# One pair of half parts moved from the expert loop into the tail's branch

## The chip, the cores and the metric

The kernel runs on one core of a Trainium2 chip. A core has five engines with queues of their own: TensorE (PE in the profile; PEld is its weight load), VectorE (DVE), ScalarE (ACT), GpSimd (POOL) and SyncE (SP), which here issues nearly all of the loads. [...] The metric is the device time of one execution in microseconds (us); for the kernel before it is the median of three runs, 2620.4 us (2619.55 to 2623.47).

## The reference

Two stages follow each other. The first is a gated attention unit on 8 sequences of 2496 tokens with width 256: scores from `z` (64 wide), a squared relu in place of a softmax, and a gate `u`. The second sends each of the 19968 tokens to one of 8 experts, by a hash of its id, and applies that expert's two layers:

```python
scores = scale * np.matmul(z, z.transpose(0, 2, 1))
attn = np.maximum(scores, 0.0) ** 2
x = (u * np.matmul(attn, v)).reshape(N, D)            # N = 19968, D = 256
expert_idx = token_ids * np.int64(2654435761) % np.int64(E)   # E = 8
for e in range(E):
    mask = expert_idx == e
    h = np.maximum(x[mask] @ w1[e], 0.0)              # w1[e]: 256 x 1024
    out[mask] = h @ w2[e]                             # w2[e]: 1024 x 256
```

The multiplier is 1 modulo 8, so the expert is the id modulo 8. Inputs come from a fixed seed, all in float32.

## The kernel before

Attention fills the first 1510 us or so and isn't touched. While it runs, the token ids are sorted into slots: `places()` counts the tokens of each expert and gives each token a row in `x_rows`, in DRAM. `idx` holds, for each slot, the token that sits in it, or N (19968) for an empty slot; a store with N as its row is dropped.

The slots are divided into units of work of three kinds:

- 32 whole blocks (`NW`) of 512 tokens of one expert (work numbers 0 to 31),
- 27 parts (`NP`) of 128 tokens of one expert (32 to 58),
- pairs of half parts of 64 tokens, where each half has an expert of its own (59 and on). With `NH` = 8 halves there are four pairs in the loop, 59 to 62. `MH` = 9 halves can be needed at most, so one more pair, 63, is in the branch.

Which expert a unit has is read on the device (`eb_i`). A number that the device also computes, `extra`, says how far the units are used: twice the number of parts (27 at least) plus the number of half parts, and N more if tokens of the first block came too late and it has to be redone. Units are thus counted in halves: the 27 parts are the first 54, and a part beyond the 27th takes both halves of a pair.

For a unit the steps are:

1. `load_x` (L699): four loads of its rows on SP. There are three buffers (`LOADS`), used in turn.
2. `load_w` (L717, L718): per expert, one read of `eb_i`, four loads for `w1` (256 KB each) and one for `w2` (1024 KB), all on SP. There are four sets of weight buffers (`w_buf`); `w_free` is a list from which a unit takes one set per expert, and into which it puts them back when its down products are written. A pair takes two sets.
3. `turn_x` (L730): VectorE transposes x.
4. The up product: `ups` for a whole block (L834) or `ups_of_part` (L855). ScalarE and VectorE take turns with the relu (L840, L842). For a part or a pair the result lies the wrong way round, and sixteen transposes on VectorE (L861) follow.
5. `down` (L869): the down product, a copy on ScalarE (L877) and a store by GpSimd (L882) with the token numbers as rows.

`run()` works through a list of units. In step i it issues the x load of unit i+2, the up product of unit i with the turn of unit i+1's x after its second bank, the down product of unit i-1, and the weight load of unit i+2. If unit i-1 is a part, its down product comes after all of unit i's up product; if it is a whole block and unit i a part, the up product of the part comes first. The first step of a call of `run` has no down product of an earlier unit. The order of instructions on each engine is the order in which this code issues them (`tc.manual_schedule()`).

The list alternates whole blocks with parts and pairs: 31 couples and then whole block 31. The first call of `run` does all but the last three units, with the loads of the next two. Then the number is read into registers of four engines, and a branch (L938) does, only when more than 62 halves are used, a second run of block 0 and the pair 63; their outputs go to `o_all`, which is cleared beforehand (L811) and stored after the branch in any case (POOL isn't in the branch). Last, the three remaining units are run.

Of the kernel before, what the change touches and what calls it, by code (L numbers as in the profile page):

```python
# [24 lines left out]
def kernel(  # L25
# [10 lines left out]
    nc = tc.nc  # L36
# [8 lines left out]
    P = 128  # L45
# [16 lines left out]
    BLK = 512  # L62
    HALF = P // 2
    NW = -(-(N - E * (BLK - 1)) // BLK)
    NP = (N - NW * BLK) // P - 1
    NH = E

    MH = max(NH, (N - NW * BLK + E * (HALF - 1)) // HALF - 2 * NP)
    NT = NP + -(-MH // 2)
# [615 lines left out]
    AHEAD = 1  # L685
    LOADS = 3
# [3 lines left out]
    def slots(j):  # L690

        return (j * BLK // P, BLK // P) if j < NW else (NW * BLK // P + j - NW, 1)

    def load_x(j, k):

        c, n = slots(j)
        xg[j] = xg_buf[k][:, 0:n * P // Q, :]
        for r in range(NQ):
            nc.sync.dma_start(  # L699
                xg[j][ts(r, Q)],  # L700
                x_dram[ds(c * P, n * P), ts(r, D // NQ)].rearrange("(k i) d -> i k d", i=Q))

    def experts(j):

        k = j - NW - NP
        return [j] if k < 0 else [*range(j + k, min(j + k + 2, NB))]

    def load_w(j):
        sets[j] = [w_free.pop(0) for _ in experts(j)]
        w1[j], w2[j] = [], []  # L710
        for k, x in zip(sets[j], experts(j)):
            w1[j].append(w_buf[k][0].rearrange("p (h f) -> p h f", h=DP))
            w2[j].append(w_buf[k][1].rearrange("p (c d) -> p c d", c=FP))
            e = nc.sync.value_load(eb_i[0:1, x:x + 1], min_val=0, max_val=E - 1)
            for r in range(NQ):
                rows = moe_w1[ds(e, 1), ts(r, D // NQ)].rearrange("one d f -> (one d) f")
                nc.sync.dma_start(w1[j][-1][ts(r, Q), :, :], rows.rearrange("(h i) f -> i h f", i=Q))  # L717
            nc.sync.dma_start(  # L718
                w2[j][-1], moe_w2[ds(e, 1)].rearrange("one f d -> (one f) d").rearrange("(c p) d -> p c d", p=P))

    def turned_x(tile, k):
        return tile[:, ts(k, XW), :].rearrange("p c d -> p (c d)").rearrange("p (k h i) -> p k h i", h=DP, i=Q)

    def turn_x(j, k):
        n = slots(j)[1] * P // Q
        xT[j] = xT_buf[k][:, 0:n]
        if slots(j)[1] == 1:

            xT[j] = xT[j].rearrange("p k h i -> p (k h i)").rearrange("p (h k i) -> p k h i", h=DP, i=Q)
        nc.vector.transpose(xT[j], xg[j].rearrange("p k (h i) -> p k h i", i=Q))  # L730
# [77 lines left out]

    opool = pool("opool", 4)
    o_all = vpool.tile([P, T, D], F32, name="v_sb")  # L810
    nc.gpsimd.memset(o_all[:, 0:BLK // P * AHEAD + (MH - NH + 1) // 2, :], 0.0)  # L811
    xT_buf.append(turned_x(o_all, T // XW - 1))

    w_free.append(len(w_buf))
# [48 lines left out]
    def down(j, t, later):  # L863
        ps = acc_ps.tile([P, D], F32, name="o_ps", tag="acc")
        for f in range(FP):
            for h, w in enumerate(w2[j]):

                cols = halves(j, h)
                nc.tensor.matmul(ps[cols, :], hT[j][f][:, ts(t, P)][:, cols], w[:, f, :],  # L869
                                 start=(f == 0), stop=(f == FP - 1), skip_group_check=True)  # L870
        k = slots(j)[0] + t
        if later is not None:
            o = o_all[:, len(later), :]
            later.append((o, again[:, k:k + 1] if j < AHEAD else idx[:, k:k + 1]))
        else:
            o = opool.tile([P, D], F32, name="o_sb")[:]
        nc.scalar.copy(o, ps[:])  # L877
        if later is None:
            store(o, once[:, k:k + 1] if j < AHEAD else idx[:, k:k + 1])
# [8 lines left out]
    def run(work, first, last, loads, later=None):  # L888

        for i in range(first, last + 1):  # L890
            if i < last and i + 2 < loads:
                load_x(work[i + 2], (i + 2) % LOADS)
            do = [lambda t=t: down(work[i - 1], t, later) for t in range(slots(work[i - 1])[1])] if i > first else []
            banks = [*range(BLK // P * 2 if work[i] < NW else 2)] if i < last else []
            if first < i == AHEAD:

                while do:
                    do.pop(0)()
            up = (ups_of_part if work[i] >= NW else ups)(work[i]) if i < last else None

            late = i > first and work[i - 1] >= NW
            for k in banks:
                next(up)
                if k == (banks[-1] if i < AHEAD else 0 if i == AHEAD else 1) and AHEAD <= i + 1 < max(last, loads):
                    turn_x(work[i + 1], (i + 1) % LOADS)
                if k % 2 == 1 and not late:
                    for _ in range(-(-len(do) * 2 // (len(banks) - k + 1))):
                        do.pop(0)()
            if i < last:
                next(up, None)  # L910
            for f in do:
                f()
            if i > first:
                w_free.extend(sets.pop(work[i - 1]))
            if i < last and i + 2 < loads:
                load_w(work[i + 2])
# [3 lines left out]

    NU = NP + NH // 2
    assert NU == NW - 1 and NH % 2 == 0 and MH <= NH + 1
    small = [*range(NW, NW + NP)]
    for k in range(NH // 2):
        small.insert((k + 1) * NU // (NH // 2 + 1), NW + NP + k)
    work = [j for pair in zip(range(NW - 1), small) for j in pair] + [NW - 1]
    NM = len(work) - 3
    load_w(work[1])  # L930
    load_x(work[1], 1)
# [1 line left out]
    n_used = nc.values_load(extra[0:1, 0:1], min_val=1, max_val=NB + N, engines=[  # L933
        mybir.EngineType.PE, mybir.EngineType.Activation, mybir.EngineType.DVE, mybir.EngineType.SP])

    nc.gpsimd.drain()  # L936
    later = []
    with tc.If(n_used > 2 * NP + NH):  # L938
        for j in [*range(AHEAD), *range(NW + NU, NW + NT)]:
            load_x(j, (NM + 2) % LOADS)  # L940
            load_w(j)
            turn_x(j, (NM + 2) % LOADS)
            run([j], 0, 1, 0, later)
    for o, rows in later:
        store(o, rows)
    run(work, NM, len(work), len(work))
# [30 lines left out]
```

## Time and profile before

| what | value |
|---|---|
| median of three runs | 2620.4 us |
| the profiled execution, its own time | 2619.45 us |
| its span, first to last instruction | 2617.4 us |
| TensorE busy | 2610.0 us, 8105 matmul records |
| VectorE, ScalarE, GpSimd busy | 1453.5, 584.2, 607.4 us |
| granted TensorE clock, whole span | 1.000 |
| DMA, mean over the span | 124 GB/s |
| one whole block and one part, per round of the loop | 34.43 us |

A float32 matmul leaves two records in the trace, so a whole block's down product of 32 matmuls is shown with x64. Matmuls are pipelined and the ends of their records are modelled, so a record reaches past the start of the next; distances between starts are the better measure. In a row of the timeline the bracket tells how long the engine had been idle before and what ended that. Queues of a transfer are named by the engine that issues it (SPq). A transfer's landing time is counted from its issue.

In the text below, a gap is time in which TensorE could have gone on but waits.

### The profile page before, as it was taken

The numbers are of one execution on the slowest core, as the hardware profiler recorded it, in microseconds if no ns is written. First come the engines' busy times: TensorE is split into PE (matmuls) and PEld (weight loads), VectorE is DVE, ScalarE is ACT, GpSimd is POOL, SyncE is SP. The second block draws the span as 40 slices with busy tenths as digits, with TensorE's granted clock in tenths as the row PEclk, the third lists the DMA queues.
The fourth block names the chain that finished last, engine by engine and source line by source line (L and its number), as shares of the span: only waits on it lengthen the run. The fifth ranks groups of instructions, "written<-read, shape, count | busy, mean of one in ns | idle before, by whom it ended". The sixth has DMA issues, their size and how long they took to land.

```text
span 2617.4 us, 26062 instructions
## 1 busy us (share of the span) xinstructions
PE 2610.0 (100%) x8105; PEld 1441.9 (55%) x8105; DVE 1453.5 (56%) x3285; ACT 584.2 (22%) x1268; POOL 607.4 (23%) x668
## 2 busy tenths in 40 slices
PE   9999999999999999999999999999999999999999
PEld 4444444444454444444444456666666666666666
DVE  7977768767766866767758633333333333333332
ACT  5214213232233123133142111111111111111111
POOL 1342233133242331333222211111111111111112
PEclk9999999999999999999999999999999999999999
DMA  4443333333422423323423387667657667667641
GB/s 121 121 120 83 84 98 93 89 95 88 117 71 77 124 71 98 102 75 95 118 55 87 104 208 182 153 165 203 162 144 196 166 159 187 152 161 198 171 126 48
DMA packets 446556, 324.91 MB, mean 124 GB/s; under 512 B 267308, under 2 KB 408765, under 8 KB 446416
## 3 DMA queue, kind: packets, MB, share of 16 engines
q1 hardware_dynamic: 424672, 281.48, 42.2%
q0 software_dynamic: 20592, 41.09, 4.9%
q8 instruction: 65, 1.06, 0.2%
q10 hardware_dynamic: 1152, 0.66, 0.1%
q14 instruction: 75, 0.61, 0.1%
HBM read 233.29 MB, written 66.75 MB: 115 GB/s over the span
## 4 chain that ended last, share of the span: by engine, by line
PE 58%; issue 35%; POOL 6%; DMA 0%; POOLq 0%; DVE 0%; ACTq 0%; DVEq 0%
PE acc L359 49%; PE s_ps L232 7%; POOL out_dram L882 6%; PE acc L367 2%; POOLq L882 0%; PE z_ps L176 0%; DMA zn<-in_z_dram 0%; DMA x_way<-x_q 0%; DMA x_sb<-x_way 0%; POOL x_rows L637 0%; DVE hT L842 0%; DVE x_sb L395 0%; POOLq L972 0%; POOLq L936 0%; POOL v_sb L811 0%
## 5 line engine op out<-in xcount | busy, mean ns | idle before, releaser
L359 PE MATMUL acc<-a,v_sb 128*128 128x512 f32 (+1 forms) x1760 | 765.9, 592 | 0.0
L270 DVE STREAM_TRANSPOSE m<-a 32x512 f32<-32x512 f32 (+1 forms) x896 | 603.8, 674 | 18.8 <-ACT a L248 3.4
L359 PEld LDWEIGHTS acc<-a,v_sb 128*128 128x128 f32 x1760 | 342.2, 196 | 390.5 <-issue 375.2
L359 PE MATMUL acc<-m,v_sb 128*128 128x512 f32 (+1 forms) x1280 | 527.2, 571 | 0.0
L842 DVE TENSOR_SCALAR hT<-h_ps 128x512 f32<-128x512 f32 x159 | 109.8, 691 | 684.5 <-PE h_ps L834 494.4
L869 PE MATMUL o_ps<-m,hT 128*128 128x256 f32 (+1 forms) x2064 | 446.9, 379 | 0.0
L240 ACT ACTIVATE a<-s_ps 128x512 f32<-128x512 f32 (+3 forms) x456 | 202.1, 585 | 1034.3 <-PE s_ps L232 1034.3
L869 PEld LDWEIGHTS o_ps<-m,hT 128*128 128x128 f32 (+1 forms) x2064 | 382.3, 188 | 75.9 <-issue 24.3
L359 PEld LDWEIGHTS acc<-m,v_sb 128*128 128x128 f32 x1280 | 251.2, 196 | 271.7 <-issue 268.2
L834 PE MATMUL h_ps<-v_sb,m 128*128 128x512 f32 x832 | 361.4, 592 | 0.7 <-PEq L938 0.7
L882 POOL DMA_INDIRECT out_dram<-o_sb,idx x155 | 151.5, 977 | 905.2 <-ACT o_sb L877 897.3
L395 POOL TENSOR_TENSOR x_sb<-x_sb,u_sb 128x256 f32<-128x256 f32 (+1 forms) x156 | 108.0, 720 | 909.3 <-DMA x_sb<-x_way 909.3
L296 DVE STREAM_TRANSPOSE a<-a 32x128 f32<-32x128 f32 (+2 forms) x1360 | 282.2, 239 | 9.9
L834 PEld LDWEIGHTS h_ps<-v_sb,m 128*128 128x128 f32 x832 | 158.0, 190 | 189.7 <-issue 188.5
L248 ACT ACTIVATE a<-a 128x512 f32<-128x512 f32 (+1 forms) x480 | 229.5, 640 | 0.0
L861 DVE STREAM_TRANSPOSE hT<-hT 32x256 f32<-32x256 f32 x496 | 214.9, 433 | 6.5
L375 DVE STREAM_TRANSPOSE x_q<-acc 128x512 f32<-128x512 f32 (+1 forms) x80 | 56.6, 708 | 281.3 <-PE acc L359 281.2
L877 ACT COPY o_sb<-o_ps 128x256 f32<-128x256 f32 x159 | 59.2, 372 | 585.6 <-PE o_ps L869 585.6
L232 PE MATMUL s_ps<-zT 64*128 64x512 f32 (+1 forms) x960 | 188.4, 536 | 0.0
L840 ACT ACTIVATE hT<-h_ps 128x512 f32<-128x512 f32 x159 | 94.8, 597 | 392.6 <-PE h_ps L834 349.7
L637 POOL DMA_INDIRECT x_rows<-x_sb,slot_i x160 | 157.8, 986 | 69.4 <-issue 35.8
L625 POOL DMA_INDIRECT slot_tokens<-token,addr x160 | 155.9, 974 | 50.9 <-issue 48.2
(121 smaller groups left out, 926.4 us busy)
## 6 DMA issues: line engine op xcount, KB each, us to landing
m<-in_moe_w_dram SPq DMA_DIRECT2D x204, 256.0 KB, 6.0
m<-in_moe_w_dram SPq DMA_DIRECT2D x51, 1024.0 KB, 6.0
m<-stage SPq DMA_DIRECT2D x320, 64.0 KB, 2.0
v_sb<-in_v_dram SPq DMA_DIRECT2D x32, 512.0 KB, 4.8
u_sb<-in_u_dram SPq DMA_DIRECT2D x32, 512.0 KB, 4.9
x_way<-x_q SPq DMA_DIRECT2D x128, 128.0 KB, 2.5
x_sb<-x_way SPq DMA_DIRECT2D x32, 512.0 KB, 4.0
v_sb<-x_rows SPq DMA_DIRECT2D x128, 128.0 KB, 6.6
```

The source lines that it names most:

```text
L232: nc.tensor.matmul(ps[:, lo:n], zT[b][h, ts(t, P)], zT[b][h, ds(g * G * P + lo, n - lo)], start=True, stop=True)
L240: nc.scalar.activation(a, ps[:, lo:n], AF.Relu)
L248: nc.scalar.activation(a, a, AF.Square, scale=1.0 / S)
L270: nc.vector.transpose(o, x[ts(r, Q), 0:m * G, ts(c, Q)].rearrange("p (i s) q -> p i s q", s=G))
L296: return n * Q, lambda: nc.vector.transpose(out, in_)
L359: nc.tensor.matmul(acc[h][:, 0:queries(g)], v_sb[b][:, t, h::2], squares(b, g, t), start=(k == 0), stop=(k == TM - 1), skip_group_check=True)
L625: st = nc.gpsimd.indirect_dma_start(out=slot_dram[:, None], out_offset=bass.IndirectOffsetOnAxis(ap=addr[0:n, c:c + 1], axis=0), in_=token ...
L637: st = nc.gpsimd.indirect_dma_start(out=x_dram[:, :], out_offset=bass.IndirectOffsetOnAxis(ap=slot_i[0:width(c % T), c:c + 1], axis=0), in ...
L834: nc.tensor.matmul(ps[:], w1[j][0][:, c, ts(f, P)], xT[j][:, :, c, :], start=(c == 0), stop=(c == DP - 1))
L861: nc.vector.transpose(turned[ts(c, Q), :, ts(r, Q)], rows[ts(r, Q), :, ts(c, Q)])
L869: nc.tensor.matmul(ps[cols, :], hT[j][f][:, ts(t, P)][:, cols], w[:, f, :], start=(f == 0), stop=(f == FP - 1), skip_group_check=True)
L882: st = nc.gpsimd.indirect_dma_start(out=out[:], out_offset=bass.IndirectOffsetOnAxis(ap=rows, axis=0), in_=o, in_offset=None, bounds_check ...
```

## The change

Pair 62, the last of the four pairs of the loop, is taken out of it. It gets an outer branch of its own in the tail, entered when more than 60 halves are used; the branch over 62 halves, with block 0 and pair 63, is put inside of it. The pair's x and weights are loaded and its x is turned ahead of the branch, whether it is entered or not. Its output goes to `o_all`, which gets one more row, and is stored with the others after the branch.

The loop's list becomes 30 couples and then whole blocks 30 and 31. The three remaining pairs are spread anew over it. The last three units, which run after the branch, were whole block 30, a part and whole block 31; now they are a part, whole block 30 and whole block 31.

```diff
-    nc.gpsimd.memset(o_all[:, 0:BLK // P * AHEAD + (MH - NH + 1) // 2, :], 0.0)
+    nc.gpsimd.memset(o_all[:, 0:BLK // P * AHEAD + (MH - NH + 1) // 2 + 1, :], 0.0)
...
-    NU = NP + NH // 2
-    assert NU == NW - 1 and NH % 2 == 0 and MH <= NH + 1
+    last_pair = NW + NP + NH // 2 - 1
+    NU = last_pair - NW
+    assert NU < NW and NH % 2 == 0 and MH <= NH + 1
     small = [*range(NW, NW + NP)]
-    for k in range(NH // 2):
-        small.insert((k + 1) * NU // (NH // 2 + 1), NW + NP + k)
-    work = [j for pair in zip(range(NW - 1), small) for j in pair] + [NW - 1]
+    for k in range(NH // 2 - 1):
+        small.insert((k + 1) * NU // (NH // 2), NW + NP + k)
+    work = [j for pair in zip(range(NU), small) for j in pair] + [*range(NU, NW)]
     NM = len(work) - 3
...
     later = []
-    with tc.If(n_used > 2 * NP + NH):
-        for j in [*range(AHEAD), *range(NW + NU, NW + NT)]:
-            load_x(j, (NM + 2) % LOADS)
-            load_w(j)
-            turn_x(j, (NM + 2) % LOADS)
-            run([j], 0, 1, 0, later)
+    load_x(last_pair, (NM + 2) % LOADS)
+    load_w(last_pair)
+    turn_x(last_pair, (NM + 2) % LOADS)
+    with tc.If(n_used > 2 * NP + NH - 2):
+        run([last_pair], 0, 1, 0, later)
+        with tc.If(n_used > 2 * NP + NH):
+            for j in [*range(AHEAD), *range(last_pair + 1, NW + NT)]:
+                load_x(j, (NM + 2) % LOADS)
+                load_w(j)
+                turn_x(j, (NM + 2) % LOADS)
+                run([j], 0, 1, 0, later)
     for o, rows in later:
         store(o, rows)
     run(work, NM, len(work), len(work))
```

## Prediction

> **What bounds the kernel now.** I read the page's busy times first, then TensorE's waits, then the timeline in order of time: a usual stretch, the tail, and what the stores of the pairs moved. Busy time:
>
> ```profile
> PE 2610.0 (100%) x8105; PEld 1441.9 (55%) x8105; DVE 1453.5 (56%) x3285; ACT 584.2 (22%) x1268; POOL 607.4 (23%) x668
> ```
>
> TensorE (PE) is busy for all but 7.4 of 2617.4 us. Its waits (engine and line, for whom, us in total, times, longest):
>
> ```profile
> PE warm L652 <- POOL zero L102: 1.2, 1, 1.2
> PE h_ps L834 <- PEq L938: 0.7, 1, 0.7
> PE z_ps L176 <- DMA zn<-in_z_dram: 0.5, 1, 0.5
> ```
>
> Two are at the kernel's start. In 1,100 us of expert work there is one, 0.7 us at the branch of L938, so TensorE's own stream sets the end: an edit gains by taking matmuls out of it and costs by opening a gap in it. Now a pair of half parts among its neighbours (start us, us, engine, line, what):
>
> ```profile
> 1716.66 13.90 PE L834 MATMUL h_ps<-v_sb,m 128*128 128x512 f32 x32
> 1730.40 3.62 PE L869 MATMUL o_ps<-zT,hT 128*128 128x256 f32 x16
> 1733.94 3.65 PE L855 MATMUL h_ps<-m,v_sb 128*64 128x512 f32 x16
> 1737.53 14.08 PE L869 MATMUL o_ps<-m,hT 128*128 128x256 f32 x64
> 1751.44 13.90 PE L834 MATMUL h_ps<-v_sb,zn 128*128 128x512 f32 x32
> 1765.27 3.67 PE L869 MATMUL o_ps<-m,hT 128*64 128x256 f32 x32
> ```
>
> A pair's up product (1733.94) and its down product (1765.27) lie 31 us apart, with 28 us of a whole block's matmuls between. What that cover hides is in the tail, where a part goes the same way:
>
> ```profile
> 2532.03 13.98 PE L869 MATMUL o_ps<-m,hT 128*128 128x256 f32 x64
> 2532.24 0.69 DVE L842 TENSOR_SCALAR hT<-h_ps 128x512 f32<-128x512 f32 x1 [6.19 <-PE h_ps L855]
> 2532.84 1.24 DVE L730 STREAM_TRANSPOSE v_sb<-v_sb 128x1024 f32<-128x1024 f32 x1
> 2534.00 7.13 DVE L861 STREAM_TRANSPOSE hT<-hT 32x256 f32<-32x256 f32 x16
> ...
> 2545.85 3.62 PE L869 MATMUL o_ps<-zT,hT 128*128 128x256 f32 x16
> 2550.17 13.97 PE L834 MATMUL h_ps<-v_sb,m 128*128 128x512 f32 x32 [0.70 <-PEq L938]
> ```
>
> After the up product VectorE needs a relu, the turn of the next block's x, and sixteen transposes until 2541.13; only then may the down product start. TensorE does a whole block's down product meanwhile.
>
> **Is the pair needed with this data?** I counted by the kernel's rules from the reference's fixed inputs. Tokens per expert: 2506, 2446, 2582, 2478, 2498, 2473, 2434, 2551. The 32 whole blocks fall 4, 4, 5, 4, 4, 4, 4, 3, leaving 458, 398, 22, 430, 450, 425, 386, 1015. Parts, (rest+63)>>7: 4, 3, 0, 3, 4, 3, 3, 8, so 28; half parts (the next lower bit): 0, 1, 1, 1, 0, 1, 1, 0, so 5. The number that the branch tests is 2x28+5 = 61. The old test, over 62, fails (as the trace shows), so no block is redone. The new outer test, over 60, holds; the inner, over 62, fails. The pair's body runs. The trace backs the counts: the pairs should hold 119, 14+22, 46+41 and 2 tokens, at 1 KB a row 0.12, 0.04, 0.09 and 0.00 MB. The software queue in the 11 us or so after each pair's down product (packets, MB, share):
>
> ```profile
> q0 software_dynamic: 48, 0.12, 2.6%
> ...
> q0 software_dynamic: 48, 0.04, 1.0%
> ...
> q0 software_dynamic: 48, 0.09, 2.0%
> ...
> q0 software_dynamic: 48, 0.00, 0.3%
> ```
>
> So the change removes no matmul. It moves a pair out of a covered place.
>
> [...] the same 128x256 shape that takes 379 ns later takes
>
> ```profile
> L652 PE MATMUL warm<-zero x6: 634/634/796, 1.2 to 3.5; 128*128 128x256 f32 x6
> ```
>
> [...] TensorE's took 236 ns here, 3.4 us ahead of the matmuls that it follows, hidden.
>
> **The change, part by part.**
>
> *Removed from the loop.* The pair with its slots: two rounds took 34.78 (1716.66 to 1751.44) and 34.79 us against 34.43 with full parts, so a pair costs 34.78+34.79-2x34.43 = 0.71 more than a part, whose two products are 3.43+3.45: 7.6 us. All of it comes back in the tail: net 0. The three other pairs move to other rounds, with the same cover: 0.
>
> *Loads moved ahead of the branch.* SP issues the pair's four x loads and twice four w1 loads and one w2, after all loads of the loop. The first expert takes the weight buffers of the block before the last one run, so only its w2 waits, for that part's down product (my t=0, 2528.4 in the old trace). Behind it on SP stand the second expert's w1 loads: issued from about t=1.7 to 4.9 (gap 0.96 from x loads to w1, and 3.17 for four, at 2515.01). 2 MB at the 220 GB/s seen in these stretches land by about t=11; TensorE comes for them at t=13.9, when the last block's down product ends. Cover 3 us; if it fails, each us late costs one. The second w2 waits for that down product, is issued at about 14.3 and, with 6.0 us to land, is there at 20.5; needed at 26. The pair's x is turned before that on an idle VectorE (0.45 us). 0 in all.
>
> *The exposed body.* Between up and down product now stands nothing. From the old tail: the relu starts at 2532.24, the transposes can follow 0.60 later (no turn of x between) and take 7.13, to 2539.97; I add 0.3 for signal and first weight load (two weight loads took 0.41 here). TensorE could have gone on at 2532.03: 8.24 us of gap. Nothing else on VectorE or ScalarE stands in it.
>
> *The clock.* [...] and 0 if the clock doesn't drop. I take 2.0.
>
> *Tail's order.* One pair fewer makes the rest after the branch part, whole, whole instead of whole, part, whole. The part has no down product to overlap: the next whole block's up product needs its x turned, which VectorE does after the part's relu: 2532.84+1.24+0.3 = 2534.38 against 2532.03, 2.35 us of gap. It was under a 14 us down product before. The part's own transposes (7.13) now hide under that up product (13.9): 0. The last block's x (after VectorE's pass through the branches, t=26) and weights (after TensorE's, t=32) land by about 47, needed after 55: 0. The rest has the old matmuls and the old end.
>
> *Branches.* The skipped inner branch takes over the old 0.70. The entered outer one runs ahead under matmuls; its exit jump I put at 0.2 (0 to 1.5).
>
> *One store more and a memset of 1536 instead of 1280 elements* on POOL (0.98; 1.2 x 1536/1280 = 1.44): POOL was idle 3.27 us after the memset, and stores are no one's wait. 0.
>
> Sum: 8.24+2.35+2.0+0.2 = +12.8. Profiled span 2617.4+12.8 = 2630.2, the profiled time 2619.45+12.8 = 2632.2. The shown median, 2620.4, is 0.95 above the profiled run: forecast 2633.2.
>
> **Rivals.**
> *No clock drop*: the gaps alone, +10.8, 2631.2. For: no gap of this length in the trace shows a drop, [...]. Against: [...] the slow first matmuls. Chance 0.18.
> *A late transfer or fetch too*: the second w1 lands 3 us or more after t=13.9, [...]: +15 to +20, 2638. For: w2 landings of 9.8 us stand in the busy stretches. Chance 0.14.
> *The body isn't run* (the other side): had the number been 60 or less, 7.6 us of matmuls go and 2.35 of the new order come: -5.2, 2615.2. It decides at 60; my count is 61, one above, and 2 tokens of one expert make it so. The last queue line can't tell 2 rows from none. Chance 0.04.
> *Covered after all*: gaps under 5 us, as when the down product is let start earlier. Nothing in the order of instructions allows it. Chance 0.02.
>
> **How the numbers follow.** The forecast has 0.62. The bound between no change and change is 0.2%, 5.2 us, about what a measurement can tell. Gaps without any cold loss, less 2 for the medians' scatter, give 2629; [...] and a little of the late case 2638.5. Outside: the two cases below, and half of the late one. Slower: 0.62+0.18+0.14 = 0.94; same 0.02 and faster 0.04 from the last two.
>
> **What would show it.** In the new trace: L855 and L869 with 128*64 shapes beside each other in the tail, with a gap near 8.2 us ended by VectorE L861; the 128*64 down product longer than 3.67 (cold); a gap of 2.35 before L834 ended by VectorE L730; one 0.7 at the inner branch; no wait for a transfer. I am wrong if those 128*64 rows are missing in the tail, or if TensorE waits for in_moe_w.

## The result and the profile after

The changed kernel takes 2633.34 us (median of six runs, 2631.89 to 2635.55) against 2620.1 for the kernel before (six runs). The ratio is 1.0047, with a 95% interval of 1.0037 to 1.0058: 13.2 us slower. The forecast was 2633.2; its sum was 12.8.

TensorE has the same 8105 records; its busy time grew by 3.6 us and the span by 14.4. The page's busy times of the kernel after:

```profile
PE 2613.6 (99%) x8105; PEld 1442.9 (55%) x8105; DVE 1453.2 (55%) x3285; ACT 584.2 (22%) x1268; POOL 607.9 (23%) x668
```

TensorE's waits (for whom: us in total, times, longest) have four rows of the tail where one stood before:

```profile
PE o_ps L869 <- issue: 4.5, 1, 4.5
PE o_ps L869 <- DVEq L944: 2.5, 1, 2.5
PE h_ps L834 <- issue: 2.1, 1, 2.1
PE acc L359 <- DVE x_q L375: 1.8, 1, 1.8
...
PE h_ps L855 <- PEq L944: 1.1, 1, 1.1
```

The row of L359 belongs to attention, which the change doesn't touch; over the traces below that wait lies anywhere from 0 to 3.6 us. So traces are compared here by their expert stage alone: from the start of the first L834 to the start of the last block's down product. Before that is 1084.88 us (1513.52 to 2598.40; the last row of 80 records, from 2594.95, starts with the part's 16, 3.45 us). After it is 1097.83: 12.95 more.

TensorE's tail after, in order of time (start us, us, line, what, and in brackets the idle time before it and what ended that):

```profile
2543.86 3.65 PE L855 MATMUL h_ps<-m,v_sb 128*64 128x512 f32 x16
2552.07 1.08 PE L869 MATMUL o_ps<-m,hT 128*64 128x256 f32 x2 [4.55 <-issue]
2555.64 5.77 PE L869 MATMUL o_ps<-m,hT 128*64 128x256 f32 x30 [2.49 <-DVEq L944]
2562.55 3.67 PE L855 MATMUL h_ps<-m,v_sb 128*128 128x512 f32 x8 [1.14 <-PEq L944]
2568.33 13.97 PE L834 MATMUL h_ps<-v_sb,zn 128*128 128x512 f32 x32 [2.11 <-issue]
```

VectorE in the same stretch:

```profile
2547.59 0.69 DVE L842 TENSOR_SCALAR hT<-h_ps 128x512 f32<-128x512 f32 x1 [19.60 <-PE h_ps L855]
2548.39 7.20 DVE L861 STREAM_TRANSPOSE hT<-hT 32x256 f32<-32x256 f32 x16
...
2566.98 1.25 DVE L730 STREAM_TRANSPOSE v_sb<-v_sb 128x1024 f32<-128x1024 f32 x1
```

The pair's rows (128*64) stand beside each other. The sixteen transposes end at 2555.59, and TensorE goes on at 2555.64. One lone couple of records at 2552.07 needs only the first eight transposes (the first half's columns); the next matmul is of the second half and waits for all sixteen, so nothing is gained. The row at 2562.55 follows the inner branch; the one at 2568.33 follows VectorE's turn of x, which ends at 2568.23, and hands over to the part's down product at 2582.14. The brackets name the branch's queue (L944) and `issue`, not VectorE's L861 and L730 that the prediction had listed as signs; it is the times of the VectorE rows that tie the two gaps to them.

The clock in this stretch (from:to, us, TensorE busy, records, granted clock, DMA share, GB/s):

```profile
2547.00:2549.80 2.80, 0.52 (x4) 0.98 0.83 294
...
2555.80:2559.80 4.00, 4.00 (x20) 0.50 0.59 134
2560.00:2563.00 3.00, 1.86 (x13) 1.00 0.18 24
```

It drops to half at 2549.68, 2.2 us after TensorE ran out of work (2547.45), and is back at 2559.92, 4.3 us after TensorE went on. The pair's down product pays for it.

### The profile page after: what moved, and what is told of

The parts are those of the page before. It is cut to its first block, busy times and chain, and to the rows that moved or that the text cites. A ratio compares the mean times of both kernels' runs of the same rounds, so it can differ in the third digit from the quotient of the medians.

```text
span 2631.8 us, 26069 instructions
## 1 busy us (share of the span) xinstructions
PE 2613.6 (99%) x8105; PEld 1442.9 (55%) x8105; DVE 1453.2 (55%) x3285; ACT 584.2 (22%) x1268; POOL 607.9 (23%) x668
## 5 line engine op out<-in xcount | busy, mean ns | idle before, releaser
L359 PE MATMUL acc<-a,v_sb 128*128 128x512 f32 (+1 forms) x1760 | 765.9, 592 | 0.0
L359 PEld LDWEIGHTS acc<-a,v_sb 128*128 128x128 f32 x1760 | 342.2, 196 | 390.5 <-issue 378.2
L359 PE MATMUL acc<-m,v_sb 128*128 128x512 f32 (+1 forms) x1280 | 527.6, 571 | 1.8 <-DVE x_q L375 1.8
L869 PE MATMUL o_ps<-m,hT 128*128 128x256 f32 (+1 forms) x1968 | 429.3, 382 | 7.0 <-issue 4.5
L869 PEld LDWEIGHTS o_ps<-m,hT 128*128 128x128 f32 (+1 forms) x1968 | 365.4, 188 | 80.0 <-issue 29.0
L359 PEld LDWEIGHTS acc<-m,v_sb 128*128 128x128 f32 x1280 | 251.0, 196 | 274.0 <-issue 268.0
L834 PE MATMUL h_ps<-v_sb,m 128*128 128x512 f32 x768 | 334.1, 592 | 0.0
L834 PEld LDWEIGHTS h_ps<-v_sb,m 128*128 128x128 f32 x768 | 145.8, 190 | 173.2 <-issue 171.7
L861 DVE STREAM_TRANSPOSE hT<-hT 32x256 f32<-32x256 f32 x496 | 214.9, 433 | 6.6
L375 DVE STREAM_TRANSPOSE x_q<-acc 128x512 f32<-128x512 f32 (+1 forms) x80 | 56.5, 706 | 284.2 <-PE acc L359 274.8
```

The source lines that it names most:

```text
L359: nc.tensor.matmul(acc[h][:, 0:queries(g)], v_sb[b][:, t, h::2], squares(b, g, t), start=(k == 0), stop=(k == TM - 1), skip_group_check=True)
L834: nc.tensor.matmul(ps[:], w1[j][0][:, c, ts(f, P)], xT[j][:, :, c, :], start=(c == 0), stop=(c == DP - 1))
L861: nc.vector.transpose(turned[ts(c, Q), :, ts(r, Q)], rows[ts(r, Q), :, ts(c, Q)])
```

## The experiments

The theory is that of the prediction: the pair costs by what used to cover it, in four terms (its chain, the clock, the order of the tail, the way out of the branch), and not by control flow or late loads. Each timed run has the kernel before timed beside it; differences are of these medians, and behind them stands the difference in the expert stage of one trace. Beside the first four runs the kernel before took 2621.96 us, 1.9 more than the 2620.1 from which their stated times start.

**The pair left out.** Is the body really entered, and what do loads and branch cost without it?

```diff
-    with tc.If(n_used > 2 * NP + NH - 2):
+    with tc.If(n_used > 2 * NP + NH):
         run([last_pair], 0, 1, 0, later)
```

> The outer test is set to over 62, so the body is not entered and the pair, with its 2 tokens, is left out of the computation; loads, branch and the tail's order are those of the change. Theory (the exposed pair costs, the rest is free but for the order of the tail): 7.6 us of matmuls go from before, 2.35 us of waiting for the turn of x stay, so 2620.1 - 7.6 + 2.35 = 2614.9 us, with TensorE's clock at 1.00 throughout. Rival (the loads put ahead of the branch or the branch's control flow cost some us by themselves): 2617 us or more.

2617.04 against 2621.96 us: ratio 0.998 (0.9972 to 0.9988), 4.9 us faster; 5.2 in the expert stage. TensorE after the branch, the pair left out:

```profile
2547.51 3.67 PE L855 MATMUL h_ps<-m,v_sb 128*128 128x512 f32 x8 [0.88 <-PEq L942]
2553.16 13.97 PE L834 MATMUL h_ps<-v_sb,zn 128*128 128x512 f32 x32 [1.98 <-issue]
```

Passing by costs 0.88 at the branch and keeps the gap of the order, 2.2 us here. The pair's 7.6 us, less this gap and the 0.18 by which the branch is longer than before, make the 5.2. With the same data, then, the number is over 60 and not over 62, and the matmuls of the pair are worth what the rounds of the loop said. The bare 2617.04 meets the rival's 2617 as well; the rival, some us for loads and branch, is out by the differences, which leave nothing for it.

That the clock would be 1.00 throughout did not hold: in attention TensorE waits 3.2 us for L375, and the clock is 0.50 from 172.86 to 176.28. In the tail it is 1.00. The fifteen executions fall in two groups, seven from 2613.56 to 2615.98 us with a mean clock of 1.000 and eight from 2617.04 to 2619.35 with 0.999; the traced one is of the second.

**The order of the tail put back.**

```diff
     NM = len(work) - 3
+    work[NM:NM + 2] = work[NM + 1], work[NM]
```

> The change, with the three units after the branch in the old order: whole block 30, the part, whole block 31. Theory: the wait of L834 for the turn of x (5.78 us from the part's up product to the whole block's, where 3.43 is usual) goes, and nothing else: 2633.3 - 2.35 = 2631.0 us. Rival (the 2.35 us are an after-effect of the slow clock or of the branch, and come wherever the tail begins): 2633.3 us, with a gap elsewhere.

2632.84 against 2621.96: 10.9 us slower instead of 13.2; 9.94 instead of 12.95 in the expert stage. The tail of that kernel:

```profile
2557.33 5.54 PE L869 MATMUL o_ps<-m,hT 128*64 128x256 f32 x30 [2.95 <-DVEq L945]
2563.85 13.97 PE L834 MATMUL h_ps<-v_sb,m 128*128 128x512 f32 x32 [0.98 <-PEq L945]
```

The gap ahead of L834 is only the branch's now; the slow down product stayed. So the order made the 2.35 us, and the rival, a gap elsewhere, is out. Of the other 0.66 us, 0.39 are this trace's shorter down product (5.54 for 5.77) and branch (0.98 for 1.14). The medians, with an interval of 8 to 15 us, can't tell this kernel from the change; the traces can, as the three of the change lie 12.69 to 14.21 above before.

**TensorE kept at work in the pair's gap.**

```diff
-        run([last_pair], 0, 1, 0, later)
+        for _ in ups_of_part(last_pair):
+            pass
+        busy = mm_ps.tile([P, D], F32, name="busy", tag="mm")
+        for _ in range(17):
+            nc.tensor.matmul(busy[:], zero[:, 0:P], zero[:], start=True, stop=True)
+        down(last_pair, 0, later)
+        w_free.extend(sets.pop(last_pair))
```

> The change, with 17 matmuls on zeros (128x256, some 7.3 us at full clock) between the pair's up and down product, where TensorE has nothing to do. Theory (the down product of 5.77 us is slow by the clock, which drops in the gap): the clock stays at 1.00, the down product takes 3.67, the gap's end does not move, and the time is 2633.3 - 2.1 = 2631.2 us. Rival (it is slow because of its own waits, two halves and two experts): 5.8 us again and 2633.3 us, or later if the added matmuls run over.

2632.8 against 2621.96: 10.8 us slower, again with an interval of 8 to 15; 10.09 in the expert stage, 2.9 less than the change. TensorE with the added matmuls (L947):

```profile
2546.98 7.61 PE L947 MATMUL busy<-zero 128*128 128x256 f32 x34
2554.51 4.32 PE L869 MATMUL o_ps<-m,hT 128*64 128x256 f32 x32
2559.48 3.67 PE L855 MATMUL h_ps<-m,v_sb 128*128 128x512 f32 x8 [0.65 <-DMA v_sb<-x_rows]
```

and its clock behind them, at full speed as in all that stretch:

```profile
2553.00:2556.00 3.00, 2.99 (x18) 1.00 0.00 0
```

The down product takes 4.32 us with the wait for the second half's transposes in it, so the clock was what made it slow. From the pair's first matmul (2543.39) to the part's it is 16.09 us here and 18.69 in the change; 2.1 of the 2.6 are the clock, the rest the way out of the branch (0.65 instead of 1.14), of which no run tells the cause (the profile puts this one down to a load of `x_rows`).

**The outer branch removed.**

```diff
-    with tc.If(n_used > 2 * NP + NH - 2):
+    if True:
         run([last_pair], 0, 1, 0, later)
```

> The change without the outer branch: the pair is worked on in the tail in any case; the inner branch stays. Theory (entering the branch is free, only the place in the order costs): 2633.3 us, 0.4 less at most; the same gap of 8.1 us and the slow down product. Rival (the nested control flow, [...]is part of the loss): 2631 us or less.

2633.32 against 2621.96: 11.4 us slower, with runs from 2631.4 to 2637.26; 12.25 in the expert stage. The pair's down product:

```profile
2553.97 5.81 PE L869 MATMUL o_ps<-m,hT 128*64 128x256 f32 x30 [2.49 <-DVEq L944]
```

Gap and slow down product are there without the branch. The part follows after 0.62 us instead of 1.14, and the whole stage is 0.7 shorter than in that trace, 0.44 shorter than in the shortest of the change: the branch accounts for no more than this, where 0.4 was stated, and the medians can't tell it.

**The change again.**

> The change itself once more, beside the kernels of this call. Every theory: 13 us above the kernel before of the same call (0.5%), with the gap of 8.1 us, the slow down product and the 2.35 us before L834 again; only TensorE's short waits in the attention stage may differ.

2633.19 against 2619.32: ratio 1.0054 (1.004 to 1.0068), 13.9 us slower; 14.21 in the expert stage, 1.26 more than in the first trace. The last rows show where from:

```profile
2559.76 3.67 PE L855 MATMUL h_ps<-m,v_sb 128*128 128x512 f32 x8 [1.64 <-PEq L944]
2565.54 15.67 PE L834 MATMUL h_ps<-v_sb,zn 128*128 128x512 f32 x32 [2.11 <-issue]
```

The whole block's up product takes 15.67 instead of 13.97 us, which no expectation had: the clock dropped a second time, at 2566.12, 0.6 us after the short gap had ended.

**The kernel before with a part first after the branch.** The pair stays in the loop.

```diff
     NM = len(work) - 3
+    work[NM:NM + 2] = work[NM + 1], work[NM]
```

> The kernel before with only the order of its last three units changed: a part, whole block 30, whole block 31, where it was whole, part, whole. The pair stays in the loop. Theory (a part that comes first leaves the next block's turn of x uncovered): 2.35 us more than before, as a gap ahead of L834 that VectorE L730 ends, and no drop of the clock. Rival (the gap needs the pair and its branch): the time of before, within 0.3 us in the trace.

2622.46 against 2619.32: ratio 1.001 (1.0002 to 1.0018), 3.1 us slower; 4.05 in the expert stage of the trace.

```profile
2555.50 15.67 PE L834 MATMUL h_ps<-v_sb,m 128*128 128x512 f32 x32 [2.11 <-issue]
```

The gap came as expected: 5.78 us from the part's up product (2549.72) to this row, where 3.43 is usual, 2.35 more. That the clock would stay did not hold: from 2555.85 to 2559.26 it is 0.50, and the up product is 1.7 us longer. 2.35+1.7 is the 4.05. The rival, no effect without the pair, is out.

**Order and clock together.** The two edits at once.

> The change with the old order of the last three units and the 17 added matmuls. Theory (the terms are independent and add up): 13.1 - 2.35 - 2.5 leaves 8.2 us above before, which is the pair's own chain of relu and sixteen transposes. Rival (the terms share a cause, so that taking both away gives less than their sum): 10 us above before.

2627.05 against 2619.32: ratio 1.0032 (1.002 to 1.0044), 7.7 us slower; 7.86 in the expert stage. The terms add up. What is left:

```profile
2544.28 7.61 PE L948 MATMUL busy<-zero 128*128 128x256 f32 x34
2551.82 4.32 PE L869 MATMUL o_ps<-m,hT 128*64 128x256 f32 x32
```

is the time that the added matmuls only pass, 7.54 us from start to start, and 0.65 by which the down product is longer than its usual 3.67, as it waits for the second half. The two make 8.19, the gap of the change: the chain of relu and transposes.

**A covered version.** Two branches, with the next units' up products between them, and block 30's turn of x ahead:

```diff
     turn_x(last_pair, (NM + 2) % LOADS)
+    turn_x(work[NM + 1], (NM + 1) % LOADS)
     with tc.If(n_used > 2 * NP + NH - 2):
-        run([last_pair], 0, 1, 0, later)
+        for _ in ups_of_part(last_pair):
+            pass
+    load_x(work[NM + 2], (NM + 2) % LOADS)
+    for _ in ups_of_part(work[NM]):
+        pass
+    for k, _ in enumerate(ups(work[NM + 1])):
+        if k == 1:
+            turn_x(work[NM + 2], (NM + 2) % LOADS)
+    down(work[NM], 0, None)
+    w_free.extend(sets.pop(work[NM]))
+    load_w(work[NM + 2])
+    with tc.If(n_used > 2 * NP + NH - 2):
+        down(last_pair, 0, later)
+        w_free.extend(sets.pop(last_pair))
         with tc.If(n_used > 2 * NP + NH):
...
     for o, rows in later:
         store(o, rows)
-    run(work, NM, len(work), len(work))
...
```

In place of the last `run` stands what it still had to do: block 31's up product with block 30's down product between its banks, and block 31's down product.

> The pair stays under the outer test, but in two branches: its up product ahead of the part's and whole block 30's up products, its down product behind them; the turn of block 30's x is put ahead of the branch. Theory (only missing cover costs): the transposes hide under 17 us of matmuls, the clock stays at 1.00, and what is left is some 0.4 to 0.5 us for each way out of a branch and up to 1.3 us where VectorE's relus of block 30 queue behind two times sixteen transposes: 1.5 us above before, 0.5 to 2.5. Rival (a conditional pair costs by its control flow and its late loads): 5 us or more above before.

2618.35 against 2619.32: ratio 0.9997 (0.9989 to 1.0006), no difference that can be told; 0.10 in the expert stage. The clock is 1.00 in every stretch.

```profile
2540.75 7.28 PE L855 MATMUL h_ps<-m,v_sb 128*64 128x512 f32 x24
2547.87 13.90 PE L834 MATMUL h_ps<-v_sb,zn 128*128 128x512 f32 x32
...
2569.62 3.67 PE L834 MATMUL h_ps<-v_sb,m 128*128 128x512 f32 x8 [0.80 <-ACTq L960]
```

The first row is both up products, of the pair and the part: 7.12 us to the next, where the two take 3.59+3.43 before, so the first branch costs 0.1. Block 30's up product (13.73 to the next) shows nothing of the queue on VectorE that I had allowed 1.3 us for. The 0.80 stands where the old branch's 0.70 stood. I had put the whole at 1.5 above before, 0.5 to 2.5: it does better.

**The covered version without the pair**, both of its tests set to over 62:

> The covered version with both of its tests set to over 62, so that the pair, with its 2 tokens, is left out: what that version gives on data that doesn't need the pair. Theory (with cover, the pair's matmuls are all that it costs): 7.6 us below before, and no gap over 1.5 us in the tail, so no drop of the clock. Rival (two branches passed by cost some us, as the change did when it was passed by): 5 us below before or less.

2610.7 against 2618.8: ratio 0.9969 (0.9958 to 0.998), 8.1 us faster; 7.05 in the expert stage. TensorE waits 0.40 and 0.55 us behind its two branches.

So on data that doesn't need the pair this version would give what the pair's matmuls cost, and on this data it costs nothing that can be measured.

**Three more traces**, to see whether a short gap always drops the clock.

> The kernel before with the part first after the branch, once more, for its trace alone. Theory (a gap of 2.35 us drops the clock in some executions and not in others, as its place against a running window decides): the gap is 2.3 to 2.4 us again, and the up product behind it takes either 13.8 us or 15.5. Rival (in this kernel the drop comes always, from something other than chance): 15.5 us again, whatever the place.

> As the other look at this kernel: a gap of 2.3 to 2.4 us, and an up product behind it of either 13.8 or 15.5 us. Theory: over the looks at these kernels both lengths occur. Rival: one and the same in each.

> The change, for its trace alone. Theory: the clock drops in the gap of 8.1 us in every execution, 2 to 6 us after the last matmul, and is back 2.5 to 4.5 us after the next; behind the gap of 2.35 us the up product takes 13.8 us or 15.5. Rival (one drop in an execution rules out the next): 13.8 us behind the second gap.

Both traces of the kernel before with a part first show 2.35 us of gap and a row of 15.67 us again, the expert stage 4.02 and 4.05 longer. The change, 12.69 longer, shows 5.77 us from the part's to the block's up product and the usual row behind it:

```profile
2568.09 13.97 PE L834 MATMUL h_ps<-v_sb,zn 128*128 128x512 f32 x32 [2.11 <-issue]
```

In the three traces of the change the long gap drops the clock every time, the short one once (in the first repeat, so one drop doesn't rule out the next). In this last one the clock is back 5.1 us after work goes on, later than the 4.5 stated. In the kernel before with the part first the short gap drops the clock in all three traces, as the rival had it.

The traces also show what decides. The record of the granted clock changes only at the ends of steps of 3.41 us: it stays at half for one, two or three of them (3.41, 6.83 or 10.24 us), and the steps lie differently against the program in each execution. Here are two steps around the short gap, in the repeat of the change, where the clock drops, and in its first trace, where it doesn't (columns as above):

```profile
2562.71:2566.12 3.41, 1.30 (x4) 1.00 0.98 198
2566.12:2569.54 3.42, 3.42 (x6) 0.50 0.85 255
```

```profile
2563.34:2566.75 3.41, 2.88 (x7) 1.00 1.00 231
2566.75:2570.16 3.41, 1.83 (x5) 1.00 1.04 253
```

In the first pair the gap lies whole within one step, in the second the end of a step divides it. So it is in all nine traces that have a gap of 2.2 to 2.4 us at this place: in the four with a drop one step holds the whole gap and 1.31 us of work; in the other five (the change twice, the pair left out, the added matmuls, no outer branch) the emptier step still holds 1.81 to 2.32 us of work. That was the theory stated for these traces: the place of the gap decides. Nor does the kernel with the part first always drop the clock: four of its thirteen timed executions have a mean clock of 1.000, so they lost less than 1.3 us to it (half a thousandth of 2621), where one step at half costs 1.7. Its three drops of three are then no more than the places that those traces drew, and the rival is out. No run moved the steps on purpose; the rule rests on the agreement of the traces.

## Why the prediction was right

*That the pair is needed.* The 128*64 rows are in the tail, and raising the test by two takes them away: the number is 61 or 62, as the count of 61 had it.

*The exposed body*, 8.24 us: 2543.86+3.59 is 2547.45, the moment at which TensorE could have gone on; it does at 2555.64, so 8.19. The chain was read from a part in the old tail, and it was the same chain. That the sum is right to 0.05 is partly luck: the step from relu to transposes took 0.80 instead of 0.60, the hand-over at the end 0.05 instead of 0.3. What I missed is harmless: the first half's matmul may start after eight transposes. TensorE did none of the part's up product in the gap: that starts at 2562.55, behind the pair's down product.

*The clock*, 2.0 us (the prediction's cold loss): 5.77 instead of 3.67 us, 2.1. The 2.0 was an estimate that the old trace doesn't show: it has no such gap, and its slow first matmuls (634 ns instead of 379) lie before 7.1 us, where its record of the clock begins, so they don't tell at what clock they ran. The runs bear the term out for this gap. A whole step without work wasn't needed: in the step ahead of the drop (2546.27 to 2549.68) TensorE still works for 1.25 us. In the other two traces of the change the same row takes 5.03 and 6.16 us, so the term is 1.4 to 2.5.

*The tail's order*, 2.35 us: 5.78-3.43 is 2.35, and 2.2 to 2.4 in every trace that has the gap. The step said nothing of the clock there, and that was incomplete: such a gap can drop it as well, and then costs 1.7 us more.

*The branches*, 0.2 us beyond the old 0.70, an estimate that nothing measured stood behind: 1.14-0.70 is 0.44 in this trace, and 0.06 to 0.94 in the other two. The outer branch did run ahead under matmuls: TensorE's compare-and-branch took 92 ns (236 at the old branch), 3.4 us before the pair's first matmul.

*Put at nothing, rightly*: the loads ahead of the branch (TensorE's waits name no in_moe_w, and the pair's up product follows at once at 2543.86), the weights of the last block, the store, the memset.

8.19+2.1+2.35+0.44 is 13.1, against the stated 12.8 and the 12.95 of the expert stage; attention's stray wait of 1.8 us, less 0.3 at the kernel's start, makes the rest of the 14.4 in the spans. That the median was met to 0.1 us is luck: the sum is 0.4 short of the measured 13.2, the kernel before came out 0.3 below the start of the forecast, and executions of the change lie from 2631.89 to 2635.55.

The rivals fell one by one: the clock did drop, TensorE waited for no transfer in the tail of the change, the body was entered, and nothing covered it.

## What to carry to other kernels

Work that is moved behind a test keeps its cost and loses its cover. Before moving it, find what runs between its dependent steps now; here 28 us of a neighbour's matmuls hid an 8 us chain, and putting the next units' up products between the pair's steps brought all 13 us back, with two branches. Count with the real data whether the test will be true: a threshold one below the number makes a saving into a loss. And look at the first unit after a seam: with no earlier unit to overlap, an order that is free in the loop may open a gap.

## What the runs showed of the hardware

The granted clock changed only at the ends of steps of 3.41 us, and its changes went with how long TensorE had worked in the step just over. In the tails of the fourteen traces, up to the last matmul, every step at full clock with 1.31 us of work or less was followed by half clock (nine steps), and none with 1.7 or more was (work as the profile shows it, with modelled ends). There, a step at half clock was followed by full clock when it held 2.78 us of work or more, and not when it held 1.67 or less. So 2.1 us of idle time were enough when they fell within one step, at a loss of 1.7 us, half a step, and the same idle time cost nothing more when the end of a step divided it.

What the gap of 8.2 us cost differed with the steps too. In the five traces that have it unfilled the clock fell 2.2 to 5.2 us after the last work and came back 2.8 to 5.1 us after work went on; half of the latter is what the pair's down product lost (in the change 2.1, 1.4 and 2.5 us for 4.3, 2.8 and 5.1). Matmuls on zeros in the gap kept it at 1.00.

A way out of a branch cost TensorE 0.1 us where the branch was entered and independent matmuls followed (the covered version), 0.4 to 0.9 where it was passed by, and 0.65 to 1.64 at the nested branch of the change.
